# A hand-written opening in another order, and one more entry in a table of steps

## The chip, the cores and the metric

The kernel runs on one core of one Trainium2 chip. The metric is the device time of one execution in microseconds. Before the change three runs took 766.13, 766.79 and 767.28 us, so the median is 766.79 us.

## What is computed

Eight batches of 3200 rows. First a gated attention with a squared ReLU in place of the softmax, then a token mixer that is linear in the sequence length once two matrices are multiplied in the right order:

```python
scores = (1 / S) * z @ z.T                 # z: 3200 x 64 in each batch
x = u * (max(scores, 0) ** 2 @ v)          # u, v: 3200 x 256
wq, wk = x @ w_q, x @ w_k                  # 256 x 64 each
out = max(wq @ (wk.T @ x) / 8, 0) @ w_out  # 256 x 256
```

The first product, 3200 x 3200 weights by 3200 x 256 values in each batch, is nearly all of the work.

## The kernel before, in words

**Tiles.** The rows of a batch are 25 blocks of 128. A *group* is the set of output rows that are accumulated together: six groups of 512 rows and a last one of 128, written (batch, group) below, with (6, 5) for group 5 of batch 6. A *tile* of scores is one block of 128 keys by the 512 queries of a group. Because the score matrix is symmetric, some tiles are turned by a DMA instead of computed again (`turned`, tiles named `tt` and `ts` in the profile). Tiles are numbered through the whole kernel and made in pairs.

**A pair's way.** `scores` (line 307 in the profile) makes two tiles in one PSUM slot, one on the upper and one on the lower half of the PE array's rows. `first_stage` takes the ReLU out of PSUM into a tile `g`, on ACT (L319) or on DVE (L321). `second_stage` squares `g` into the fp16 tile `at`, on ACT (L330) or on POOL (L332). `second_product` multiplies `at` with `v` into the two accumulators `acc` (L369). There are three PSUM slots of the pool `pps`, which scores share with every other product that is not the accumulation.

**The opening.** z of batch 0 is loaded on the SP queue in four pieces (`ZCH`: 4, 6, 7 and 8 blocks). The string `OPENING` (line 78) is an order written out by hand, one word for each action, and `opening` (line 989) issues them. The letter is the action, the first digit the piece or the pair, and the last letter the engine (A is ACT, D is DVE, P is POOL):

- `z20P` casts half 0 of piece 2 to fp16 (L121); both halves of a piece are cast
- `t2` turns piece 2 on PE (L130); `c2D` copies what was turned into the fp16 tile `zT` (L136)
- `s2` is `scores` of pair 2; `e2D` its first stage; `q2A` its square; `m2` its second product
- `w10` is 20 matmuls on zeros (L981), which fill the time before the first piece is there
- `v1` is a load of part of v, issued from POOL (L112)

Each engine does its own words in the order of the string. Pairs 0 and 1 need piece 0 only, pairs 2 to 4 need piece 1, pairs 5 to 7 need piece 2.

**The steps.** Behind the opening a loop (`while groups`, line 1028) does one step k after another, from k = 3 on. A step makes new scores, mostly three pairs (`n = 6` tiles), squares the pairs of the step before, and multiplies rows of one group with v. One block of 128 keys is called a *row* of a step below. The count of rows in a step comes from a small plan at line 1113: `steps` says over how many steps what is left of the group is spread, from what has been made so far, and the rows are divided evenly. A step only uses tiles that were made at least two steps ago (`LAG`). When a group's last row is done, `gate` multiplies by u and frees the accumulators.

A step may also carry other work, in PE's time between these products:

- *keys* (`keys_and_heads`): the projection of a finished group to wq and wk, and the product wk.T @ x (the *heads*) of the group before it. Its results go through ACT (L544) and then through a DMA on the SP queue (`turn_keys`, L551: `kx<-qk`, for the last, short group `kx<-ql`). The heads that read them run with the next keys. After a batch's last heads, `turn_heads` (L610) turns the sum, which DVE has added up (L598). In the last two batches, heads of groups 5 and 6 run together.
- *mix*: `mix` (L657) multiplies two groups of wq with the heads of a batch, for one half of the 256 columns; ACT takes the ReLU (L678). A step that mixes makes two pairs instead of three, and its first stages are all on DVE.
- *projection* (`project`): the last product with w_out of one group, `fo` in the profile.

Which step does what is decided by `mix_due` and `key_due`, by due times (`between`) and by how much is waiting. The table `chosen` (line 911) overrules them for single steps: "k", "m" and "p" allow keys, mix and projection in that step.

With the table of before, the decisions of steps 142 to 154 are these ("mix 5,1,0" is batch 5, groups 2 and 3, first half of the columns):

| step | group | pairs made | rows | besides |
|---|---|---|---|---|
| 142 | 6,5 begins | 3 | 9 | projection 4,4 |
| 143 | 6,5 | 3 | 8 | keys |
| 144 | 6,5 ends | 2 | 8 | mix 5,0,0 |
| 145 | 6,6 whole | 3 | 25 (short) | projection 4,5 |
| 146 | 7,0 begins | 3 | 7 | keys |
| 147 | 7,0 | 3 | 6 | |
| 148 | 7,0 | 2 | 6 | mix 5,0,1 |
| 149 | 7,0 ends | 2 | 6 | mix 5,1,0 |
| 150 | 7,1 begins | 3 | 5 | keys of 6,5 and 6,6 |
| 151 | 7,1 | 2 | 5 | mix 5,1,1; projection 5,0 |
| 152 | 7,1 | 3 | 5 | keys of 7,0, heads of 6,5 and 6,6 |
| 153 | 7,1 | 3 | 5 | projection 5,1 |
| 154 | 7,1 ends | 2 | 5 | mix 5,2,0; projection 5,2 |

Of the kernel before, what the change touches and what calls it, by code (L numbers as in the profile page):

```python
# [16 lines left out]
def kernel(  # L17
# [56 lines left out]
    def acc_tile(half, name, dtype=FP32):  # L74
# [1 line left out]
        return pacc.tile([P, n], dtype, tag=f"acc{half}", name=name)  # L76

    OPENING = """
        v0 z00D z01A w10 t0 w2 w1 c0D z10A z11P t1 c1D v1 s0 s1 e0A v2 e1D z20P z21P q0A s2
        e2D q1A z30P z31P s3 e3A t2 m0 s4 c2D q2A v3 e4D q3P t3 m1 c3D s5 e5A q4A s6 e6D m2  # L80
        s7 e7D
    """
    ENDING = """
# [782 lines left out]
    def group_begun(k, b, gi):  # L866
# [42 lines left out]

    heading_more = {165: -1}  # L910
    chosen = {
        18: "k", 19: "p", 20: "p", 21: "m", 35: "k", 36: "p", 38: "p", 101: "p", 147: "k",
        148: "m", 149: "m", 159: "mp", 161: "p", 163: "m"
    }

    def mix_due(k):
# [104 lines left out]
    produced, consumed, k = 16, 6, 3  # L1021
# [332 lines left out]
```

## Time and profile before

| | |
|---|---|
| median of three runs | 766.79 us |
| the profiled execution's own time | 766.35 us |
| its span, first to last instruction | 764.6 us |
| PE busy (matmuls) | 753.7 us |
| DVE, ACT, POOL busy | 462.5, 549.4, 539.9 us |
| mean granted clock of TensorE | 0.999 |

The profiled execution takes 1.75 us more than its span, the time around the first and the last instruction. Rows of the timeline give the start in us, the time until the last of a merged set ends, the engine, the line, what is written and read, the count, and in brackets the engine's idle time before it with what ended it. SPq is the queue of DMA issues. A row of two or more instructions is merged, so its start is that of the first.

### The profile page before, as it was taken

The page shows a single profiled execution, that of the slowest core. Times are in us where ns is not written, and L with a number is a line of the kernel's source. Part 1 is how long each engine was busy: PE and PEld are TensorE (multiplying, and loading weights), DVE is VectorE, ACT ScalarE, POOL GpSimd, SP SyncE. Part 2 cuts the span into 40 slices and gives each one's busy share as a digit, 9 for nine tenths or more (in the row PEclk, how much of TensorE's full clock was granted, in tenths as well). Part 3 has the DMA queues.
Part 4 walks back from the last instruction along what each step waited for, and adds up shares of the span by engine and source line. Part 5 has one row for each costly group of instructions (what it writes and reads, how often), then busy time and mean ns, then how long its engine had stood idle before and what let it go on. Part 6 is the DMA issues. An engine that isn't in the chain of part 4 may idle for free.

```text
span 764.6 us, 29066 instructions
## 1 busy us (share of the span) xinstructions
PE 753.7 (99%) x12888; PEld 618.7 (81%) x12888; DVE 462.5 (60%) x457; ACT 549.4 (72%) x649; POOL 539.9 (71%) x354
## 2 busy tenths in 40 slices
PE   9999999999999999999999999999999999999996
PEld 6777888888888887888888888888878888878884
DVE  7654675546755567555665557655566555755534
ACT  7666776677767777687776877759777697776555
POOL 7897797768766678676887668866688666854540
PEclk9999999999999999999999999999999999999999
DMA  9999889998999979996999999899999998998627
GB/s 176 191 197 222 187 195 181 141 215 151 206 185 214 239 182 181 233 258 163 214 186 210 259 178 185 154 224 252 153 213 188 218 271 162 163 218 178 178 71 265
DMA packets 289615, 150.24 MB, mean 196 GB/s; under 512 B 265168, under 2 KB 268752, under 8 KB 289488
## 3 DMA queue, kind: packets, MB, share of 16 engines
q1 hardware_dynamic: 288768, 146.48, 93.8%
q0 software_dynamic: 576, 1.64, 1.1%
q8 instruction: 100, 1.64, 0.9%
q14 instruction: 27, 0.22, 0.1%
q10 hardware_dynamic: 144, 0.26, 0.1%
HBM read 59.38 MB, written 26.21 MB: 112 GB/s over the span
## 4 chain that ended last, share of the span: by engine, by line
PE 96%; DVE 1%; ACT 1%; issue 0%; DMA 0%; DVEq 0%; ACTq 0%
PE acc L369 72%; PE sc L307 12%; PE fo L369 5%; PE qk L369 5%; PE mx L657 1%; DVE x_sb L507 1%; DVE fo L1312 0%; PE sc L981 0%; DMA kx<-ql 0%; PE ztp L130 0%; PE qk L610 0%; DVE g L321 0%; PE xtx L634 0%; ACT at L330 0%; PE hd L644 0%
## 5 line engine op out<-in xcount | busy, mean ns | idle before, releaser
L321 DVE TENSOR_SCALAR g<-sc 128x1024 f32<-128x1024 f32 x330 | 402.0, 1224 | 242.2 <-PE sc L307 229.0
L332 POOL TENSOR_TENSOR at<-g 128x1024 f16<-128x1024 f32 x230 | 433.3, 1894 | 131.2 <-DVE g L321 113.3
L369 PE MATMUL acc<-v_sb,at 64*128 64x256 f16 (+1 forms) x7187 | 462.1, 269 | 2.0 <-DVE x_sb L507 0.5
L369 PEld LDWEIGHTS <-at 64*128 64x128 f16 (+1 forms) x7187 | 354.4, 94 | 86.1 <-PE acc L369 25.0
L330 ACT ACTIVATE at<-g 128x1024 f16<-128x1024 f32 x226 | 234.8, 1055 | 12.0 <-DVE g L321 6.3
L369 PE MATMUL acc<-v_sb,tt 64*128 64x256 f16 x2552 | 179.3, 269 | 0.0
L307 PE MATMUL sc<-zT 64*128 64x512 f16 (+1 forms) x1008 | 164.5, 356 | 0.6 <-ACT g L319 0.4
L319 ACT ACTIVATE g<-sc 128x1024 f32<-128x1024 f32 x126 | 129.0, 1024 | 46.5 <-PE sc L307 45.6
L369 PEld LDWEIGHTS <-tt 64*128 64x128 f16 x2552 | 130.4, 94 | 14.0
L509 POOL TENSOR_TENSOR x_sb<-gt,u_sb 128x512 f16<-128x512 f32 x48 | 61.2, 1276 | 65.0 <-ACT gt L506 61.4
L678 ACT ACTIVATE rt<-mx 128x1024 f16<-128x1024 f32 x47 | 47.9, 1023 | 34.5 <-PE mx L657 34.4
L506 ACT COPY gt<-acc 128x512 f32<-128x512 f32 x48 | 28.0, 584 | 47.0 <-PE acc L369 45.2
L307 PEld LDWEIGHTS <-zT 64*128 64x128 f16 x1008 | 51.7, 94 | 9.3 <-issue 2.4
L369 PE MATMUL fo<-wo,rt 64*128 64x256 f16 (+1 forms) x696 | 58.1, 270 | 0.0
L544 ACT CAST qk<-qk 128x512 f16<-128x512 f32 x47 | 27.5, 585 | 35.7 <-PE qk L369 33.0
L369 PEld LDWEIGHTS <-rt 64*128 64x128 f16 (+1 forms) x696 | 35.6, 94 | 15.2 <-PE fo L369 6.3
L507 DVE TENSOR_TENSOR x_sb<-acc,u_sb 128x512 f16<-128x512 f32 x48 | 33.2, 691 | 19.9 <-PE acc L369 18.6
L739 ACT ACTIVATE fo<-fo 128x1024 f32<-128x1024 f32 x39 | 39.9, 1024 | 2.4 <-PE fo L369 2.2
L369 PEld LDWEIGHTS <-x_sb 64*128 64x128 f16 x672 | 29.8, 95 | 4.7 <-PE qk L369 0.9
L369 PE MATMUL qk<-kx,x_sb 64*128 64x64 f16 x672 | 32.8, 190 | 0.0
L369 PE MATMUL qk<-xT_sb,wkq 64*128 64x512 f16 (+3 forms) x118 | 25.8, 326 | 0.0
L369 PE MATMUL qk<-xT_sb,wqk 64*128 64x384 f16 (+3 forms) x148 | 25.1, 296 | 0.0
(86 smaller groups left out, 275.3 us busy)
## 6 DMA issues: line engine op xcount, KB each, us to landing
u_sb<-in_u_dram SPq DMA_DIRECT2D x48, 512.0 KB, 5.3
out_dram<-fo SPq DMA_DIRECT2D x43, 512.0 KB, 3.9
piece<-in_v_dram SPq DMA_DIRECT2D x42, 512.0 KB, 5.2
piece<-in_z_dram SPq DMA_DIRECT2D x7, 512.0 KB, 4.9
tt<-at SPq DMA_TRANSPOSE x162, 4.7
out_dram<-fo SPq DMA_DIRECT2D x9, 256.0 KB, 2.9
piece<-in_z_dram SPq DMA_DIRECT2D x7, 288.0 KB, 4.8
u_sb<-in_u_dram SPq DMA_DIRECT2D x8, 128.0 KB, 4.8
```

The lines of the kernel that those rows point to most:

```text
L307: nc.tensor.matmul(out=sc[:, h, at : at + w], lhsT=zT[b][half : half + dqk, ds(z_at(b, h) + ti * P, P)], rhs=zT[b][half : half + dqk, ds(z ...
L319: nc.scalar.activation(out=g[:], in_=sc[:], func=RELU, scale=GSCALE)
L321: nc.vector.tensor_scalar(out=g[:], in0=sc[:], scalar1=0.0, scalar2=GSCALE, op0=AOP.max, op1=AOP.mult)
L330: nc.scalar.square(out=out, in_=g[:])
L332: nc.gpsimd.tensor_mul(out=out, in0=g[:], in1=g[:])
L369: return nc.tensor.matmul(out=self.out, lhsT=self.lhsT(rows), rhs=self.rhs(rows), start=start, stop=stop)
L506: nc.scalar.copy(out=upper[:], in_=accs[1][:])
L507: nc.vector.tensor_mul(out=x[:, 0:n], in0=accs[0][:, 0:n], in1=ug[:, 0:n])
L509: nc.gpsimd.tensor_mul(out=x[:, n : 2 * n], in0=upper[:], in1=ug[:, n : 2 * n])
L544: nc.scalar.copy(out=qks[b, gi][:, 0:gw], in_=out)
L678: nc.scalar.activation(out=out, in_=ps[:], func=RELU)
L739: nc.scalar.mul(out=flat_out[:, sl], in_=part, mul=FINAL_SCALE)
```

## The change

The opening's string is written in another order, and some words go to another engine; the table gets an entry for step 142.

```diff
     OPENING = """
-        v0 z00D z01A w10 t0 w2 w1 c0D z10A z11P t1 c1D v1 s0 s1 e0A v2 e1D z20P z21P q0A s2
-        e2D q1A z30P z31P s3 e3A t2 m0 s4 c2D q2A v3 e4D q3P t3 m1 c3D s5 e5A q4A s6 e6D m2
+        v0 z00D z01A w10 t0 w2 w1 c0D z10A s0 z11P t1 c1D s1 e0A v1 e1D v2 z20P z21D q0A s2
+        e2A q1A z30D z31P s3 e3A m0 t2 c2D q2A v3 s4 m1 e4D q3P t3 s5 c3D e5A q4A s6 e6D m2
         s7 e7D
     """
...
     chosen = {
-        18: "k", 19: "p", 20: "p", 21: "m", 35: "k", 36: "p", 38: "p", 101: "p", 147: "k",
-        148: "m", 149: "m", 159: "mp", 161: "p", 163: "m"
+        18: "k", 19: "p", 20: "p", 21: "m", 35: "k", 36: "p", 38: "p", 101: "p", 142: "mp",
+        147: "k", 148: "m", 149: "m", 159: "mp", 161: "p", 163: "m"
     }
```

Engine by engine the new opening reads:

| engine | before | after |
|---|---|---|
| PE | w10 t0 w2 w1 t1 s0 s1 s2 s3 t2 m0 s4 t3 m1 s5 s6 m2 s7 | w10 t0 w2 w1 s0 t1 s1 s2 s3 m0 t2 s4 m1 t3 s5 s6 m2 s7 |
| ACT | z01 z10 e0 q0 q1 e3 q2 e5 q4 | z01 z10 e0 q0 e2 q1 e3 q2 e5 q4 |
| DVE | z00 c0 c1 e1 e2 c2 e4 c3 e6 e7 | z00 c0 c1 e1 z21 z30 c2 e4 c3 e6 e7 |
| POOL | v0 z11 v1 v2 z20 z21 z30 z31 v3 q3 | v0 z11 v1 v2 z20 z31 v3 q3 |

## The prediction

> **What bounds the kernel now.** I read the page's head first, then the list of what PE waited for, then the timeline at the two places that the change touches.
>
> ```profile
> span 764.6 us, 29066 instructions
> PE 753.7 (99%) x12888; PEld 618.7 (81%) x12888; DVE 462.5 (60%) x457; ACT 549.4 (72%) x649; POOL 539.9 (71%) x354
> PE sc L981 <- DVE zeros L1018: 1.0, 1, 1.0
> PE qk L369 <- DMA kx<-ql: 0.6, 1, 0.6
> PE acc L369 <- DVE x_sb L507: 0.5, 3, 0.2
> PE sc L307 <- ACT g L319: 0.4, 1, 0.4
> ```
>
> PE bounds it. The change adds no product and removes none, so it can only give or take idle time of PE, and the list (us in total, times, longest) is short: the largest wait behind the opening is 0.6 us, once, on the DMA that turns the short group's keys. Two sums are therefore enough, one for the opening and one for the end of batch 6.
>
> **The opening, before.** The timeline up to 14 us, with the rows that carry the chain:
>
> ```profile
> 4.00 0.42 DVE L136 COPY zT<-ztp 128x512 f16<-128x512 f16 x1 [0.81 <-PE ztp L130]
> 4.66 0.49 PE L130 MATMUL ztp<-ident,zd 128*128 128x128 f16 x6
> 5.09 1.11 PE L307 MATMUL sc<-zT 64*128 64x512 f16 x6
> 5.19 0.56 DVE L136 COPY zT<-ztp 128x768 f16<-128x768 f16 x1 [0.77 <-PE ztp L130]
> 5.52 1.02 ACT L319 ACTIVATE g<-sc 128x1024 f32<-128x1024 f32 x1 [1.33 <-PE sc L307]
> 5.74 2.36 DVE L321 TENSOR_SCALAR g<-sc 128x1024 f32<-128x1024 f32 x2
> 5.80 0.11 PEld L307 LDWEIGHTS <-zT 64*128 64x128 f16 x3 [0.61 <-DVE zT L136]
> 6.57 2.00 ACT L330 ACTIVATE at<-g 128x1024 f16<-128x1024 f32 x2
> 7.69 1.05 PE L369 MATMUL acc<-v_sb,at 128*128 128x256 f16 x8
> 8.48 1.01 ACT L319 ACTIVATE g<-sc 128x1024 f32<-128x1024 f32 x1
> 8.67 0.39 PE L307 MATMUL sc<-zT 64*128 64x512 f16 x2
> 8.99 0.62 PE L130 MATMUL ztp<-ident,zd 128*128 128x128 f16 x8
> 9.39 1.05 ACT L330 ACTIVATE at<-g 128x1024 f16<-128x1024 f32 x1
> 9.45 1.04 PE L369 MATMUL acc<-v_sb,at 128*128 128x256 f16 x8
> 10.41 0.60 PE L307 MATMUL sc<-zT 64*128 64x512 f16 x4
> 11.93 0.82 PE L307 MATMUL sc<-zT 64*128 64x512 f16 x6
> 12.44 2.36 DVE L321 TENSOR_SCALAR g<-sc 128x1024 f32<-128x1024 f32 x2 [0.15 <-PE sc L307]
> 13.72 0.39 PE L307 MATMUL sc<-zT 64*128 64x512 f16 x2
> ```
>
> The reader is to see three things. Pair 0 begins at 5.09 although its data (c0) is there at 4.00 + 0.42 = 4.42; the turns of piece 1 stand before it. m0 waits for ACT until 7.69, with the turns of piece 2 before it. And the last hold is at 13.72, where PE waits for e7 on DVE to give back a PSUM slot. From there PE runs dense, so what the opening is worth is how far that 13.72 moves.
>
> **The opening, after**, by the same intervals.
>
> - s0 follows c0 as s2 follows c1 now (5.19 + 0.56 = 5.75, next weights at 5.80): 4.42 + 0.07 = 4.49, 0.60 earlier.
> - e0 starts 0.43 behind s0 (5.09 to 5.52): 4.92. q0 1.05 later (5.52 to 6.57): 5.97. m0 1.12 behind that (6.57 to 7.69): 7.09. So m0 gains 0.60.
> - e2 is now on ACT. ACT starts its next instruction 0.95 behind a square (two squares in 2.00, one alone 1.05) and 0.91 behind a first stage (8.48 to 9.39). So e2 starts at 6.92 and q1 at 7.83, where it stood at 7.52: the first stage that ACT took over eats the 0.60 and 0.31 more.
> - m1, again 1.12 behind q1: 8.95. PE is there at 8.68: m0 to 7.96, t2 to 8.4, s4 to 8.68. It idles 0.27.
> - m1 takes 0.87 (8 starts 0.109 apart), then t3 and the change to s5 0.54 (t1 to s0 is 0.43 for 6 turns, two more are 0.11), with 0.02 between: s5 at 10.38, against 10.41.
> - s5 to s7 holds the same words as before and takes the same 1.52 (10.41 to 11.93), if q2 is in time: e3 at 8.78, q2 at 9.69, its end and m2 at 10.80, while PE comes to m2 at 10.92. So s7 at 11.90, e7 on DVE 0.03 earlier than now, and the slot at 13.69 in place of 13.72.
>
> **The opening gives 0.03 us.** What m0 gains, m1 waits for.
>
> The other moved words cost nothing, each under a cover with a number:
>
> ```profile
> 2.90 0.29 DVE L121 CAST zd<-z 128x256 f16<-128x256 f32 x1 [1.95 <-DMA z<-in_z_dram]
> 2.90 0.41 ACT L121 CAST zd<-z 128x256 f16<-128x256 f32 x1 [0.87 <-DMA z<-in_z_dram]
> 9.57 1.89 POOL L332 TENSOR_TENSOR at<-g 128x1024 f16<-128x1024 f32 x1 [1.13 <-ACT g L319]
> v_sb<-in_v_dram POOLq DMA_DIRECT2D x1, 384.0 KB, 4.6
> ```
>
> - z21 and z30 on DVE have 448 and 512 elements a row; no row shows these. From the DVE row they are 0.51 and 0.59, by ACT's row as the other end 0.71 and 0.81; I take DVE's own. They start behind e1, which moves to 5.89 because t1 now stands behind s0 (t1 at 4.81, c1 at 5.34), and ends at 7.11. So z21 is done by 7.62 to 7.82, and t2 starts at 7.96 behind m0; z30 is done by 8.21 to 8.63, and c2 is wanted at 8.57. At the upper end c2 loses 0.06, which e4 and s6 have in hand. Without m0 as the cover, t2 would be 0.5 late.
> - q3 on POOL follows e3 and starts about 0.3 later than 9.57. Behind it on POOL stands the square of pair 5, which waits for e5 until 11.9 either way, and q3 ends at 11.8.
> - v1 stays behind z11 in POOL's queue and lands 4.6 us after its issue at 4.16, 8.8, and m2 reads it at 10.92. v3 goes 0.5 earlier because two casts ahead of it are gone.
>
> Bounds for the opening: at most 0.15 gained (q2's margin of 0.12 is the next stop), at most 0.60 lost (s0 no earlier than now, with e2 on ACT all the same).
>
> [...] The row first:
>
> ```profile
> 3.76 0.84 PE L981 MATMUL sc<-zeros 128*128 128x128 f16 x6
> ```
>
> These six start 0.107 apart, the six turns at 4.66 only 0.055 apart, at the same width: PE goes to twice its speed between 4.29 and 4.66, and s0 moves to 4.49, into that gap. [...]
>
> **The entry for step 142.** Followed through the rules of the loop:
>
> - Step 142 now mixes 5,0,0 and projects 4,4, with two pairs in place of three. The mixes that follow come at 144 (5,0,1), 148 (5,1,0), 149 (5,1,1) and, as before, 154 (5,2,0).
> - From 142 to 150 one pair fewer has been made. So at 146 the plan finds one more limit below the group's end, 823, and spreads group 7,0 over five steps of 5 rows (146 to 150) in place of four; 7,1 then has four (151 to 154: 7, 6, 6, 6 rows) in place of five.
> - Step 151 makes three pairs, not two, and catches up. From 155 all decisions are as before. Steps, mixes, keys, projections, pairs and rows in 142 to 154 are the same in number.
> - Keys of the short group stay at 150. The heads that read them go from 152 to **153**, because 7,0 ends a step later and its keys come due a step later.
>
> ```profile
> 664.78 2.21 SPq L351 DMA_TRANSPOSE tt<-at  x1
> 668.39 1.17 SPq L551 DMA_TRANSPOSE kx<-ql  x1
> 669.75 0.28 PE L369 MATMUL qk<-kx,x_sb 64*128 64x64 f16 x4
> 670.70 0.19 PE L369 MATMUL qk<-kx,xl 64*128 64x64 f16 x1 [0.64 <-DMA kx<-ql]
> 673.34 0.28 PE L610 MATMUL qk<-ident,hT 128*128 128x128 f16 x2
> DVE hT L598: 0.4, 1
> issue: 1.1, 5
> 668.60:673.50 4.90, 4.13 (x81) 3.48 (x75) 2.95 (x5) 2.63 (x4) 3.12 (x3) 1.00 0.56 143
> 654.60:657.90 3.30, 3.30 (x58) 2.56 (x56) 2.36 (x3) 2.85 (x3) 1.36 (x2) 1.00 1.16 172
> ```
>
> The rows of the stall, the waits of the heads' turn (in this window, then in the whole span), and two windows (length, then PE busy): step 152 has 4.90 us with PE busy for 4.13, step 148 is 3.30 all busy. The heads stand still 0.64 us for the key that was issued at 668.39. A step more ahead of them is over 3.3 us, five times the wait, so it goes: **-0.64**. The turn of the heads at the end of the same step waits 0.4 us for DVE; with 6 rows in step 153 in place of 5 it comes a row later (0.43, as m1 multiplies two such rows in 0.87), and what is left is the usual 0.22 of the other batches (1.1 us over 5 of them, with no releaser): **-0.20**. What is late next: the mixes of batch 6 begin at 158, so hss has four steps.
>
> Costs of the new order: two pairs and a mix instead of three pairs change which products lie side by side, and each change costs PE about 0.1 (s4 to t3 is 0.32, a pair of scores alone 0.21); the counts come out even, so 0, with 0.2 either way. Bounds of this part: -1.0 to 0.
>
> **Sum**, against the profiled execution's 766.35: -0.03 - 0.64 - 0.20 = -0.87, 765.5. The median of the runs is 0.44 above that execution, so for the median **765.9**.
>
> **The rivals.**
>
> - *s0 at half clock.* For it, s0 lies in the gap named above; against it, 4.49 is past its middle. The pair takes 0.43 in place of 0.22 and drains later: 0.25 in all. As m1 has no slack, all of it arrives at 13.72: 766.2. [...]
> - *The stall moves with the heads*, because the key is held on the SP queue by a turned tile that waits for its square. For it, a turned tile held that queue for 2.21 from 664.78 on; against it, the step's worth of time. Then only 0.03 is left: 766.8.
> - *POOL falls behind in the steps of 5 rows*, the slower side:
>
> ```profile
> 649.30 5.74 POOL L332 TENSOR_TENSOR at<-g 128x1024 f16<-128x1024 f32 x3
> 656.97 1.89 POOL L332 TENSOR_TENSOR at<-g 128x1024 f16<-128x1024 f32 x1 [1.94 <-DVE g L321]
> ```
>
> POOL squares three pairs without a pause up to 655.04, then idles 1.94. With 5 rows in place of 7, 6 and 6, steps 147, 148 and 149 start 0.9, 1.3 and 1.7 earlier, and that idle time shrinks to nothing. Step 149 now begins at 657.9, the end of the window above, so I put it at 656.2, and it reads POOL's last square 1.2 us after it ends. If POOL is later by more than that, by one more square queued ahead, say, each us is lost on PE: two squares less the slack, 3.78 - 1.2 = 2.6, give 768.5.
>
> **How the numbers follow.** Forecast 0.50, s0 at half clock 0.20, the stall moves 0.12, POOL behind 0.10, and 0.08 for a gain that I don't see, in PSUM slots handed out otherwise in the whole kernel. Runs of this kernel lie 0.07% around their median, and about 0.2%, 1.5 us, can be told from no change. The forecast and the next two lie inside that (0.82 less the tails). Slower needs POOL, or 0.6 from the opening with no gain behind it: 0.14. Faster needs more than the 1.15 that the bounds allow, plus the runs' spread: 0.18. Same: 0.68. The range takes in both bounds (-1.15 to +0.6), half the spread of the runs on top, and part of POOL's case: 764.8 to 768.0.
>
> **What would show it.** Right: q1 about 0.3 later than now with m0 near 7.1, PE's third score pair of step 3 again near 13.7; no wait on `kx<-ql` and five short steps for 7,0. Wrong: the hold at 13.7 gone or a us away; a new wait of PE on POOL's squares near 655; the wait on `kx<-ql` one step further on.

## The result, and the profile after

The changed kernel takes 765.57 us (median of 22 runs) against 766.93 us for the kernel before (22 runs), a ratio of 0.9984 with a 95% interval of 0.9978 to 0.9990. That is 1.36 us less in the medians, and inside the 0.2% that the prediction took for no change that can be told. One run of the changed kernel took 1118.34 us at a granted clock of 0.655; it is in the median and not in the ratio. The profiled execution takes 765.49 us, 0.86 less than the 766.35 of before. The prediction had 765.9 for the median, 0.9 below its three runs of before, and -0.87 for the sum. So the trace's difference is the one forecast, and the medians moved half as far again. The total came out, its parts did not, and the sections below are about that.

The head of the page, and the whole list of what PE waited for:

```profile
span 763.7 us, 29059 instructions
PE 754.3 (99%) x12888; PEld 618.0 (81%) x12888; DVE 461.9 (60%) x458; ACT 551.1 (72%) x651; POOL 537.1 (70%) x351
PE sc L981 <- DVE zeros L1018: 1.0, 1, 1.0
PE acc L369 <- DVE x_sb L507: 0.5, 3, 0.2
```

Of before's list, the wait on `kx<-ql` is gone, as planned. The 0.4 on `g` in the opening is gone too, and so is a wait of 0.3 on `gt` (DVE, L500), the smallest of that list and not among the rows that the prediction showed. PE's busy time is 0.6 longer with the same 12888 matmuls, because more of the opening's matmuls ran at half speed (the trace's record of the granted clock stands at 1.0 from 7.03 us on, before from 4.57 on; up to 14 us PE is busy for 12.77 in place of 12.15, behind it for 741.50 in place of 741.56).

The opening after, from the timeline of PE, ACT and DVE:

```profile
4.01 0.42 DVE L136 COPY zT<-ztp 128x512 f16<-128x512 f16 x1 [0.81 <-PE ztp L130]
4.55 0.61 PE L307 MATMUL sc<-zT 64*128 64x512 f16 x2
5.09 0.82 PE L130 MATMUL ztp<-ident,zd 128*128 128x128 f16 x6
5.20 1.02 ACT L319 ACTIVATE g<-sc 128x1024 f32<-128x1024 f32 x1 [0.96 <-PE sc L307]
5.84 1.54 PE L307 MATMUL sc<-zT 64*128 64x512 f16 x6
7.22 1.02 ACT L319 ACTIVATE g<-sc 128x1024 f32<-128x1024 f32 x1
7.37 1.05 PE L369 MATMUL acc<-v_sb,at 128*128 128x256 f16 x8
7.63 0.94 DVE L121 CAST zd<-z 128x448 f16<-128x448 f32 x2
8.13 1.05 ACT L330 ACTIVATE at<-g 128x1024 f16<-128x1024 f32 x1
9.23 1.05 PE L369 MATMUL acc<-v_sb,at 128*128 128x256 f16 x8
10.66 0.61 PE L307 MATMUL sc<-zT 64*128 64x512 f16 x4
12.18 0.86 PE L307 MATMUL sc<-zT 64*128 64x512 f16 x6
13.97 0.39 PE L307 MATMUL sc<-zT 64*128 64x512 f16 x2
```

s0 starts at 4.55, but its two matmuls take 0.61, where a pair at full speed takes 0.39. The six turns behind it take 0.82; the same six took 0.49 before. PE is at half speed up to 7.0 here (the pair at 6.57 takes 0.60, the next one 0.41), and e0 starts 0.65 behind s0, not 0.43. From e0 on the rows stand in the predicted intervals, all 0.28 to 0.30 later: e2 7.22 (6.92), q1 8.13 (7.83), m1 9.23 (8.95), s5 10.66 (10.38), s7 12.18 (11.90), the slot 13.97 (13.69). Against 13.72 before, this opening is 0.25 longer.

The end of batch 6: windows over the five steps of 7,0 (length, then busy us of PE, PEld, DVE, ACT and POOL), then the issue of the short group's key and three PE rows of step 153.

```profile
646.40:649.30 2.90, 2.90 (x69) 2.37 (x66) 1.65 (x2) 2.56 (x4) 1.94 (x4) 1.00 0.55 198
649.30:652.60 3.30, 3.30 (x59) 2.54 (x55) 2.92 (x4) 2.97 (x4) 3.30 (x2) 1.00 0.30 45
652.60:655.90 3.30, 3.30 (x60) 2.65 (x56) 2.58 (x3) 2.34 (x3) 2.56 (x3) 1.00 1.28 280
655.90:659.20 3.30, 3.30 (x56) 2.53 (x52) 2.80 (x3) 2.49 (x3) 2.34 (x2) 1.00 0.82 181
659.20:662.40 3.20, 3.20 (x70) 2.83 (x66) 2.48 (x3) 2.72 (x4) 2.72 (x2) 1.00 1.20 253
664.05 1.97 SPq L551 DMA_TRANSPOSE kx<-ql  x1
672.49 0.22 PE L369 MATMUL qk<-kx,x_sb 64*128 64x64 f16 x2
672.54 0.22 PE L369 MATMUL qk<-kx,xl 64*128 64x64 f16 x2
675.34 0.29 PE L610 MATMUL qk<-ident,hT 128*128 128x128 f16 x2
```

PE is busy in the whole of all five steps. POOL is full in one of them (3.30 of 3.30) and has 0.5 to 1.0 to spare in each of the others. The heads read the short group's key at 672.54, 1.84 later than before and without a wait. The key itself is issued at 664.05 in place of 668.39, so more of the new margin comes from the earlier key than from the later heads. The turn of the heads (L610) waits 0.2 for DVE in place of 0.4, as in the other batches.

The stores at the end, before and after, from the timeline of the SP queue:

```profile
747.83 13.26 SPq L1318 DMA_DIRECT2D out_dram<-fo  x14
```

```profile
746.70 12.86 SPq L1318 DMA_DIRECT2D out_dram<-fo  x14
```

The last 14 stores start 1.13 earlier; PE's last matmul ends 1.13 earlier too (758.20 to 757.07). The span ends only 0.85 earlier (764.57 to 763.72), so 0.28 is given back behind PE. Over all traces below the time behind PE's last matmul lies between 6.37 (before) and 6.81 us, so this part is in good measure the luck of two traces.

Books of the two traces: opening +0.25; the stretch around 182 us -0.37; from the gate at 346 us to the last mix 408.13 to 407.13, -1.00; behind PE +0.28. Together -0.84.

### The profile page after: what moved, and what is told of

It reads as the page before. It is cut to its first block, busy times and chain, and to the rows that moved or that the text cites. A ratio compares the mean times of both kernels' runs of the same rounds, so it can differ in the third digit from the quotient of the medians.

```text
span 763.7 us, 29059 instructions
## 1 busy us (share of the span) xinstructions
PE 754.3 (99%) x12888; PEld 618.0 (81%) x12888; DVE 461.9 (60%) x458; ACT 551.1 (72%) x651; POOL 537.1 (70%) x351
## 4 chain that ended last, share of the span: by engine, by line
PE 97%; DVE 2%; issue 0%; DMA 0%; ACT 0%; DVEq 0%; ACTq 0%
PE acc L369 72%; PE sc L307 12%; PE fo L369 5%; PE qk L369 5%; PE mx L657 1%; DVE x_sb L507 1%; DVE fo L1312 0%; DVE g L321 0%; PE ztp L130 0%; DMA z<-in_z_dram 0%; PE qk L610 0%; DVE zT L136 0%; PE xtx L634 0%; PE hd L644 0%; ACT fo L1316 0%
## 5 line engine op out<-in xcount | busy, mean ns | idle before, releaser
L330 ACT ACTIVATE at<-g 128x1024 f16<-128x1024 f32 x227 | 236.1, 1056 | 14.3 <-DVE g L321 7.2
```

The source lines that it names most:

```text
L330: nc.scalar.square(out=out, in_=g[:])
```

## The experiments

The last three columns are read from each trace: the 11th pair of scores (the "slot" of the prediction), PE's wait at 182 us, and the tail stretch, from DVE's first instruction of the gate at 346 us to the start of the last mix (L657). Each ratio is against runs of before on the same chip: their medians are 766.87 for e1 to e4, 766.67 for e5 to e8 and 766.84 for e9 to e12.

| kernel | median us | ratio, 95% interval | slot | wait at 182 | tail stretch |
|---|---|---|---|---|---|
| before | 766.93 | | 13.72 | 0.30 | 408.13 |
| after | 765.57 | 0.9984 [0.9978, 0.9990] | 13.97 | none | 407.13 |
| e1, table only | 766.24 | 0.9990 [0.9980, 1.0000] | 14.07 | 0.30 | 407.10 |
| e2, opening only | 766.41 | 0.9992 [0.9981, 1.0003] | 14.32 | none | 407.46 |
| e3, before again | 766.40, one run | | 14.06 | 0.30 | 407.73 |
| e4, heads late | 766.50 | 0.9990 [0.9980, 1.0001] | 14.30 | 0.30 | 408.03 |
| e5, before, one more on DVE | 766.79 | 1.0002 [0.9993, 1.0010] | 13.88 | none | 407.61 |
| e6, after, z21 on POOL | 766.48 | 1.0002 [0.9993, 1.0011] | 13.98 | 0.28 | 407.18 |
| e7, table, one more on DVE | 765.99 | 0.9989 [0.9979, 1.0000] | 14.38 | none | 407.13 |
| e8, after, e2 on DVE | 766.36 | 0.9997 [0.9988, 1.0006] | 14.35 | 0.29 | 407.18 |
| e9, after again | 765.32 | 0.9982 [0.9973, 0.9990] | 13.91 | none | 407.05 |
| e10, after, t1 ahead | 766.17 | 0.9994 [0.9986, 1.0003] | 13.97 | none | 407.05 |
| e11, after, one more on DVE | 765.80 | 0.9985 [0.9975, 0.9994] | 14.00 | none | 407.05 |
| e12, e8, one more on DVE | 765.39 | 0.9986 [0.9975, 0.9997] | 13.61 | none | 407.05 |

### One half of the change at a time (e1, e2, e3)

e1 is the kernel before with the new entry alone; e2 has the new opening with the old table; e3 is the kernel before, word for word.

```diff
-        18: "k", 19: "p", 20: "p", 21: "m", 35: "k", 36: "p", 38: "p", 101: "p", 147: "k",
-        148: "m", 149: "m", 159: "mp", 161: "p", 163: "m"
+        18: "k", 19: "p", 20: "p", 21: "m", 35: "k", 36: "p", 38: "p", 101: "p", 142: "mp",
+        147: "k", 148: "m", 149: "m", 159: "mp", 161: "p", 163: "m"
```

> The entry for step 142 alone, with the opening of before. Theory (the gain is the late heads): the wait of PE on kx<-ql (0.64 us before) is gone, the turn of the heads no longer waits on DVE beyond 0.2, and the time is 0.8 to 1.0 us below the kernel before, ratio near 0.9989. Rival (the two edits share the gain, the new opening gives 0.3 to 0.5 of it): only 0.7 to 0.9 of the 1.2 us between the two kernels, ratio 0.9989 to 0.9991 here and 0.9994 to 0.9996 with the opening alone.

> The new opening alone, without the entry. Theory (what m0 gains, m1 waits for): the third score pair of step 3, at 13.72 us before, comes at 13.7 if PE is at full clock by 4.5 us and 0.25 later, near 13.97, if not; the time is within 0.3 us of the kernel before, ratio 0.9996 to 1.0004, and the wait on kx<-ql of about 0.6 us is still there. Rival (the opening gains): 0.3 to 0.5 us faster, ratio 0.9994 to 0.9996.

> The kernel before once more, for a second trace. If the moment at which PE goes to full clock is a matter of chance, its first matmuls may turn fast anywhere between 4.4 and 7 us; if the change moved it, they turn between 4.3 and 4.7 us as in the first trace. If the wait on kx<-ql is made by the order of work, it is 0.6 us again; if it hangs on how fast a transposing DMA lands, it differs by some tenths. The 0.3 us wait of PE at 182 us on DVE's copy comes again if the program makes it, and is gone if it was chance.

The table alone gives 0.6 us and the opening alone 0.5, each with an interval that reaches 1.0 or past it, so neither is told from nothing by its time. The table was expected to give 0.8 to 1.0, the opening at most 0.3. e1's trace shows that the whole tail belongs to the table: 407.10 against 408.13, no wait on `kx<-ql`, heads at step 153, 0.2 at L610. e3 shows how much of before's trace is chance. PE goes to full speed at 5.2 to 5.4 us there, 0.8 later than in the first trace, and the slot is at 14.06. PE comes to the heads 0.49 later, 0.34 of it from the opening, and the wait on `kx<-ql` is then nearly gone from the list, as the key comes on the SP queue's own time (issued at 668.31, against 668.39 before). PE's rows in e3:

```profile
670.24 0.28 PE L369 MATMUL qk<-kx,x_sb 64*128 64x64 f16 x4
670.62 0.19 PE L369 MATMUL qk<-kx,xl 64*128 64x64 f16 x1
```

So before's 0.64 was a meeting of two chains, and delays of PE ahead of it were taken up by it. The idle time is also not the whole cost. One of these matmuls takes 0.19, but the four of the first row start 0.03 apart. So idle time, which counts from the end of the last one, leaves out most of that one's 0.19. From start to start the step onto the short group's key is 0.86 us before, 0.29 in e3 and 0.03 in the changed kernel. The wait cost 0.83 before, and 0.26 in e3, where its idle time is 0.07.

e2 has what e1 lacks: no wait at 182 us, which is worth 0.37 (below). e2 also shows a wait that the prediction did not have, m0 on the first part of v (PE's rows):

```profile
7.91 1.03 PE L369 MATMUL acc<-v_sb,at 128*128 128x256 f16 x8 [0.78 <-DMA v_sb<-in_v_dram]
14.32 0.39 PE L307 MATMUL sc<-zT 64*128 64x512 f16 x2
```

The 256 KB of v landed 6.4 us after their issue at 1.5, against 4.5 in the changed kernel's first trace. e8 has the same wait (0.75) and ends its opening at 14.35.

### The heads alone (e4)

```diff
     chosen = {
-        18: "k", 19: "p", 20: "p", 21: "m", 35: "k", 36: "p", 38: "p", 101: "p", 147: "k",
+        18: "k", 19: "p", 20: "p", 21: "m", 35: "k", 36: "p", 38: "p", 101: "p", 147: "k", 152: "p", 153: "k",
```

This puts the heads at step 153 and the projection of step 153 at step 152, and leaves mixes, pairs and rows as before.

> The kernel before with other entries: step 152 projects and step 153 takes the keys, no mix is moved and group 7,0 keeps its four steps. Theory (one step more between the short group's keys and the heads that read them is what counts): the wait on kx<-ql is gone and the time falls by 0.8 to 1.0 us, as with the entry for 142. Rival (the moved mixes and the five short steps matter too): the wait goes, but the time falls by less than 0.5 us.

The wait on `kx<-ql` is gone, so the heads' step is what decides it. The turn at L610 still waits 0.4 (in this version 153 has 5 rows, in the changed kernel 6), as the prediction's step had it. But a new wait stands at 682 us, and the tail is back at 408.03:

```profile
682.12 0.39 PE L307 MATMUL sc<-zT 64*128 64x512 f16 x2 [0.36 <-ACT fo L739]
```

ACT came to that `fo` straight from two squares, 679.15 to 681.15; what put them there was not followed further. The median is 0.37 below before, the rival's case. So later heads do not close the tail by themselves. Whether the new stall comes from the moved projection, or from mixes, pairs and rows that stayed, is not shown.

### What made the wait at 182 us (e5, e6, e7)

ACT and DVE each copy one half of the accumulators of a short group (L499, L500). Before:

```profile
181.27 0.37 ACT L499 COPY gt<-acc 128x256 f32<-128x256 f32 x1 [0.27 <-PE acc L369]
181.63 0.42 DVE L500 COPY gt<-acc 128x256 f32<-128x256 f32 x1 [1.16 <-PE sc L307]
182.11 2.15 PE L369 MATMUL acc<-v_sb,at 64*128 64x256 f16 x31 [0.30 <-DVE gt L500]
```

After:

```profile
181.50 0.42 DVE L500 COPY gt<-acc 128x256 f32<-128x256 f32 x1 [0.79 <-PE acc L369]
181.51 0.37 ACT L499 COPY gt<-acc 128x256 f32<-128x256 f32 x1 [0.27 <-PE acc L369]
181.98 2.27 PE L369 MATMUL acc<-v_sb,at 64*128 64x256 f16 x34
```

The copy waits for the same semaphores before and after. DVE's wait for PE, ahead of the copy, ended at 181.2 before (the row of line 500; duration, then first and last start):

```profile
L500 DVEq EVENT_SEMAPHORE  x1: 21/21/21, 181.2 to 181.2; - x1
```

The copy then stood for 0.42 us with nothing left that it waited for. Counted in DVE's records, waits included, L500 is number 192 before and number 193 after, because the new opening gives DVE one instruction more. (The expectations count one more and call these 193 and 194.) That gave the theory: it is late because of its place. e5 is the kernel before with one column of zeros written behind the others, where DVE is idle:

```diff
     nc.vector.memset(zeros[:], 0.0)
+    nc.vector.memset(spare[:], 0.0)
```

e6 is the changed kernel with one cast put back, which takes one instruction from DVE again. e7 is e1 with the memset of e5.

```diff
-  ... v2 z20P z21D q0A s2
+  ... v2 z20P z21P q0A s2
```

> The kernel before, with one more instruction on DVE at the very start (a memset of one column behind the zeros, where DVE is idle); opening and table are untouched. At 181.6 us the kernel before lets DVE's copy of the accumulators (L500) start 0.42 us after its last semaphore, and PE waits 0.30 for it; every trace with the old opening has this, none with the new one. Theory: the copy is late because of its place in DVE's own sequence of instructions (it is number 193 = 3 x 64 + 1 there, and one further on with the new opening), so one more instruction anywhere ahead of it takes the wait away: L500 starts within 0.05 us of ACT's copy (L499), the 0.30 is gone from the list of waits, and the time is 766.9 - 0.38 = 766.5, or up to 766.9 if the wait on kx<-ql takes up the gain (it was 0.64 and would then be about 1.0). Rival: the wait comes from the order of PE's and ACT's work in the old opening; then it stays at 0.30 and the time at 766.9.

> The changed kernel with one word put back: the cast z21 is on POOL as before, so DVE has one instruction less and its copy L500 is number 193 again; PE's, ACT's order and the table stay changed. Theory of the place in DVE's sequence: the wait of 0.30 at 182 us is back, L500 starts 0.36 after L499, and the time is 765.6 + 0.38 = 765.95. Rival, that PE's or ACT's order in the opening made the wait go: no wait there, 765.6. The cast itself has 0.3 us in hand on POOL ahead of t2 and should cost nothing.

> The old opening, the new entry of the table, and the one additional memset on DVE. If the place of L500 in DVE's sequence is what the new opening gained, the table alone (766.24) less 0.38 gives 765.9, and the wait at 182 is gone; what is left to the changed kernel's 765.57 is then the new opening's own worth (0.3). If the new opening is worth nothing by itself, or less, the time is 765.6 or below. Rival (the opening's order made the gain at 182): 766.2 with the wait.

The wait followed the count in all three: gone in e5 and e7, with PE's and ACT's opening as before; back in e6, with both as in the changed kernel:

```profile
181.53 0.37 ACT L499 COPY gt<-acc 128x256 f32<-128x256 f32 x1 [0.27 <-PE acc L369]
181.88 0.42 DVE L500 COPY gt<-acc 128x256 f32<-128x256 f32 x1 [1.15 <-PE sc L307]
182.35 0.29 PE L369 MATMUL acc<-v_sb,at 64*128 64x256 f16 x2 [0.28 <-DVE gt L500]
```

The stretch around it, between the gates at 161 and 239 us, is 78.18 to 78.21 us in the eight traces without the wait and 78.56 or 78.57 in the six with it, so it costs 0.37. The times were less tidy. e5 is at 766.79, no faster than before (766.67 on that chip), not the hoped 766.5; its profiled execution was the longest of its 11 runs (768.87) and holds a wait of 1.6 on a turned tile that no other trace has, and others on ACT. e6 is 0.9 above the changed kernel where 0.38 was expected; its trace has 0.55 more span and 0.27 more around it, and the rest of its median has no cause that was shown. e7 at 765.99 was expected at 765.9. Among the kernels with the new entry, the three with the wait take 766.24 to 766.48 and the six without it 765.32 to 766.17.

### What the words of the opening are worth (e8, e10, e12)

e8 puts e2 back on DVE and z21, z30, z31 on POOL:

```diff
-  ... v2 z20P z21D q0A s2
-  e2A q1A z30D z31P s3 e3A ...
+  ... v2 z20P z21P q0A s2
+  e2D q1A z30P z31P s3 e3A ...
```

e12 is e8 with the additional memset, so that the wait at 182 does not come in. e10 is the changed kernel with t1 ahead of s0 again:

```diff
-  ... c0D z10A s0 z11P t1 c1D s1 e0A ...
+  ... c0D z10A z11P t1 c1D s0 s1 e0A ...
```

> The changed kernel with the first stage of pair 2 back on DVE and the three casts z21, z30, z31 on POOL; PE's new order and the table stay. Theory that the first stage on ACT eats what m0 gains: q1 begins 1.0 behind q0 and m1 is no longer late, so the hold of step 3 (the 11th pair of scores) comes 0.3 to 0.6 earlier than in the changed kernel for the same moment of the clock, near 13.5. DVE's L500 is number 193 again, so the 0.30 at 182 is back: 765.6 - 0.3 + 0.38 = 765.7. Rival, that the clock's moment alone sets the opening and e2 has slack: the pair comes at 13.7 to 14.3, and 765.9 to 766.0.

> The changed kernel with the first stage of pair 2 back on DVE, z21, z30, z31 on POOL, and the additional memset on DVE, so that L500 is number 194 and the wait at 182 does not come in. It tells what e2 on ACT is worth alone. Theory that it eats m0's gain: q1 near 7.8 in place of 8.1, and with an early landing of v the 11th pair of scores at 13.8 to 13.9, 0.1 to 0.2 earlier than the changed kernel's; time 765.5. With a late landing m0 waits and both are at 14.3. Rival, that DVE's two first stages behind each other make pair 2 late: q1 at 8.1 or later, 14.0 or more, time 765.9.

> The changed kernel with one move undone: the turns of piece 1 (t1) again stand ahead of the first scores s0, all else as changed, e2 on ACT too. DVE's L500 stays number 194, so no wait at 182. Theory that the ACT chain e0 q0 e2 q1 without a pause sets the opening: s0 comes 0.5 later than in the changed kernel if t1 still runs at half speed, 0.4 if at full, so q1 and the 11th pair of scores come 0.4 to 0.5 later: 14.4, time 766.0. Rival, that the clock's moment makes up for it (s0 then runs at full speed, 0.28 shorter, and t1 costs nothing): 14.1, time 765.7.

In e8 v was late, m0 waited for it, and nothing could be told of e2; the wait at 182 was back as expected. In e12 v was in time and PE turned to full speed just before s0 began at 4.59:

```profile
4.59 0.39 PE L308 MATMUL sc<-zT 64*128 64x512 f16 x2
5.02 1.02 ACT L320 ACTIVATE g<-sc 128x1024 f32<-128x1024 f32 x1 [0.85 <-PE sc L308]
8.88 1.05 PE L370 MATMUL acc<-v_sb,at 128*128 128x256 f16 x8
13.61 0.39 PE L308 MATMUL sc<-zT 64*128 64x512 f16 x2
```

At full speed e0 is 0.43 behind s0, as the prediction had it, and the slot is at 13.61, the earliest of all traces. Against e9 (below), where e0 is at 5.15, m1 is 0.30 earlier (9.18 to 8.88) and so is the slot (13.91 to 13.61); 0.13 of it is e0's, so 0.17 is what e2 on ACT costs, if the casts that e12 has back on POOL cost nothing. Nothing of it shows in the time: e12's median is 765.39, between the two of the changed kernel (765.57 and 765.32).

In e10 the turn to full speed came at 4.0 us, the earliest of all, t1 took 0.49, and e0 started at 5.22 in spite of standing behind it, 0.02 later than in the changed kernel. The slot is at 13.97 in both: the clock's moment made up for the place of s0, the rival's case. Over 12 runs the median is 766.17, 0.6 to 0.85 above the changed kernel's two, which is what the theory had for s0 ahead of t1; no trace shows those slower runs, so that s0 is their cause is not shown.

### The changed kernel again, and with one more instruction (e9, e11)

> The changed kernel once more, word for word. It says which marks of its trace are its own and which are chance. Expected as its own: no wait at 182 us, the last mix 407.1 us behind the gate at 346 us, no wait on kx<-ql. Expected as chance: the moment at which PE goes to its full speed (6.6 to 7.0 us in the first trace) and the landing of the first part of v (4.5 us after its issue there, 6.4 in two other traces with the new opening, where m0 then waits 0.8 for it): the 11th pair of scores at 13.7 to 14.0 with an early landing, at 14.3 with a late one. Time 765.6 to 765.9. Rival, that the new opening's length is fixed: 13.97 again whatever the landing.

> The changed kernel with the same additional memset on DVE, so L500 is number 195. A control: if only the place of number 193 (3 x 64 + 1) is late, nothing changes: no wait at 182, time as the changed kernel's, 765.6 to 765.9. If the memset itself moved something (the clock, the landing of v), or if every place of L500 behind the boundary gained, it would show here: 766.2 or more, or 765.2 or less.

e9 has the marks expected as its own (nothing at 182, 407.05, no wait on `kx<-ql`). PE turned to full speed between 4.38 and 5.04, inside s0 (the pair took 0.48, the six turns behind it 0.51), and the slot came at 13.91.

e11 was to be a control. Its time, 765.80, is inside what was expected, but something did change: there is a new wait of 0.27 at PE's end. It is the same effect in another place. The memset moved a copy of the last product onto number 832 of DVE's records (rows of DVE, then PE):

```profile
753.89 2.36 DVE L1314 TENSOR_SCALAR fo<-fo 128x1024 f32<-128x1024 f32 x2 [0.71 <-PE mx L658]
755.17 1.03 PE L370 MATMUL fo<-wo,rt 128*128 128x256 f16 x8 [0.27 <-DVE fo L1314]
```

Its own wait ended at 753.49, and it started 0.40 later.

## Why the prediction came out

- **s0 at 4.49, 0.60 earlier.** Nearly right: 4.55, 4.63 and 4.59 in the traces of after, e9 and e12.
- **e0 0.43 behind s0.** This step failed. It took an interval at full speed for a pair that ran at half speed. The rival named this, with a slot 0.25 later than the forecast's, at a chance of 0.20; measured was 13.97 against 13.69. The row that would have warned was there: before's turn lay between 4.29 and 4.66, in one trace only. Over the twelve traces of the experiments and the two profiles it lay, by each trace's record of the granted clock, between 4.0 (e10) and 7.0 (after), a spread of 3.0 us that one trace could not show, and only in e10 ahead of 4.49, where the forecast put s0. In six of the seven traces with s0 ahead of t1 the pair took 0.48 to 0.61, against 0.39 in the seventh (e12), so half speed, in whole or in part, was the usual case, and 0.20 too little for it.
- **From e0 to the slot.** Right in every interval, to 0.02. e2 on ACT eats what m0 gains, and m1 waits for ACT; e12 shows 0.17 of it.
- **Casts on DVE.** z21 and z30 took 0.94 together, against 1.10 predicted, and cost nothing at the slot.
- **v is in time.** Wrong in two of the traces with the new order. The step looked at v1 and not at v0: when the first part lands 6.4 us after its issue, m0 waits 0.75 to 0.78 and the slot is at 14.3.
- **Entry 142.** Steps, rows and heads went as written, the wait on the key went, and the turn's fell to the usual 0.2. The tail gained 1.00 where 0.64 + 0.20 = 0.84 was predicted. The mis-sized term is the 0.64: it is idle time, and from start to start the wait cost 0.83, which with the turn's 0.20 makes 1.03. The rivals in which the stall moves with the heads, or POOL falls behind, did not come. e3 puts the size in its place: it was one meeting of PE with the SP queue. Against the first trace's tail of 408.13 the entry gains 1.00, against e3's 407.73 it gains 0.60, and about 0.2 of that is a pause of PE at 607 us in e3, ahead of the steps that the entry changes.
- **What the sum left out.** -0.37 at 182 us, for which the prediction had only "a gain that I don't see" at 0.08, by another mechanism, and +0.28 behind PE's last matmul, where it let the whole of PE's gain through. With the opening's +0.28 over the forecast and the tail's surplus of 0.16 they cancel to within 0.03 us. That the total came out is luck.

## What to carry to other kernels

Profile the same kernel two or three times before an interval of the first ten microseconds is costed: here the old opening's slot lay between 13.72 and 14.30 in four traces with no edit to it (before, e1, e3, e4): 13.72 with the clock's turn at 4.57, 14.06 with it at 5.2 to 5.4 (e3). PE's wait on the key's DMA was a meeting of two chains, 0.64 in the first trace of before and 0.07 in e3, where PE came 0.49 later, so the size of such a wait in one trace is no price: time saved ahead of it may go into the wait, and time lost ahead of it may be free. Price it from start to start of the matmuls around it (0.83 here), as its idle time (0.64) leaves out the overlap that is lost with it. Count the instructions that an edit adds to or takes from an engine: here one more on DVE took away the wait at 182 us, worth 0.37 (e5, e7), and brought one of 0.27 at PE's end (e11), so the place of the later instructions was an effect of its own, and one idle instruction more is a cheap way to test it.

## What the hardware showed that was not expected

**At places 128 apart in DVE's sequence, instructions started about 0.4 us late.** Counted in DVE's records, the places are 64, 192 and so on. Where such a place held a working instruction, DVE was idle and no other wait could hold it, it started 0.40 to 0.47 us after its own wait ended: numbers 64, 192 and 448 before (0.47, 0.42, 0.40), and 448, 576, 704 and 832 in e11 (four times 0.40). At the places half way between, numbers 128 and 256 of e5 and 384 and 640 of e11, the same distance was 0.05. In all 14 traces 3180 working instructions stand right behind a wait with DVE idle; 25 of them are at these places and 0.40 to 0.47 late, and none of the other 3155 is 0.15 behind its wait. Where the place held a wait, nothing was late: number 192 after is the wait of L500, and the copy behind it starts 0.05 after that wait's end (181.45 to 181.50). DVE's rows before at the first and the third place (their waits ended at 53.88 and 403.60):

```profile
54.34 1.23 DVE L321 TENSOR_SCALAR g<-sc 128x1024 f32<-128x1024 f32 x1 [1.37 <-PE sc L307]
404.00 1.22 DVE L321 TENSOR_SCALAR g<-sc 128x1024 f32<-128x1024 f32 x1 [1.33 <-PE sc L307]
```

PE loses nothing at these two; in that trace only the place at 182 us costs PE time.

The profile lists two DMA queues of the kind "instruction". One of them has 27 packets of 8 KB in the whole of before:

```profile
q14 instruction: 27, 0.22, 0.1%
```

One of these packets moves at 182.8, 1.2 us after the late copy before, and at 179.4 after. Whether these packets have to do with the late instruction is not shown.

**The landing of one turned tile can cost more than the change gives.** At 35 us ACT writes into a slot of `at` that a transposing DMA has to leave first. ACT's rows, before and in e12:

```profile
34.82 1.06 ACT L330 ACTIVATE at<-g 128x1024 f16<-128x1024 f32 x1 [3.55 <-DMA tt<-at]
```

```profile
36.70 1.06 ACT L331 ACTIVATE at<-g 128x1024 f16<-128x1024 f32 x1 [5.55 <-DMA tt<-at]
```

Released at 34.8, PE never notices; at 35.95 (e1) it waits 0.3, and at 36.7 (e12) 1.5. So e12 has the earliest opening of all, and its profiled execution still takes 766.50 where its median is 765.39. No version here is clearly better than the changed kernel; e12 is level with it.
